# x1 of four token tiles kept in SBUF, loads tied to tiles, and stores in the order of their loads, in an S4 + gMLP block

## The chip, the cores and the metric

The kernel runs on one core of one Trainium2 chip. The metric is the device time of one execution in microseconds, the median over the runs that were taken.

## What is computed

One block with two parts, on x of 2048 tokens by 576 channels. The first part adds an S4 long convolution to x, with a kernel made from complex poles (128 states a channel); the second adds a gated MLP that mixes along the tokens.

```python
h = layernorm(x) * (1 + ca) + sa                 # sa..gb: silu(c) @ w_mod
x = x + ga * S4(h)                               # x after this line is "x1"
h = layernorm(x) * (1 + cb) + sb
z = gelu(h @ w_in)                               # 576 -> 4608
z1, z2 = z[:, :2304], layernorm(z[:, 2304:])
g = w_sp @ z2 + b_sp[:, None]                    # 2048 x 2048 over the tokens
x = x + gb * ((z1 * g) @ w_out)                  # 2304 -> 576
```

## The kernel before

Matrices of the MLP are split into two float16 parts each (high and low), and every product is three matmuls: high x high, high x low, low x high. The rows are in an order of tokens that the convolution likes, in 16 tiles of 128 tokens.

Instructions are recorded in program order, and a scheduler places them on the engines by its own estimate of times. An instruction that goes through `pin` (`keep_in_program_order`) is held in the order in which it was written. Each engine runs its own list in order; SyncE (SP) and GpSimd (POOL) mostly issue DMAs, and an issue that has to wait holds up all that stand behind it in that queue.

**SSM.** The convolution runs by channel chunks: four of 128 channels and one of 64 (`chan(c)`). At its end, `y_load(c, q)` loads v (from `v_d`) and x of four tiles (quarter q) and `y_unit(c, q)` multiplies, adds x in place (line 507) and stores x1 to the DRAM tensor `x1_d` (line 508). The last 64 columns of x1 stay in SBUF in `x1l`, too.

**First MLP phase** (`phase_a`, lines 922 to 983). For each of 16 tiles: `ln2_rows` loads x1 (line 862, tile x1t), takes its mean and variance (line 851) and normalises it; `ln2_cols` transposes it (line 877) into nt, which is stored to `n2_d` (line 884); `z2_mm` multiplies nt with the second half of w_in, which stays in SBUF as wz (line 899), and applies GELU (line 900), in three groups per tile of up to 28 matmuls, each with one of four PSUM buffers; `z2_stats` (ending in line 908) and `z2_parts` (lines 917 to 920) normalise z2 and store its two parts (zhl) to `z2_d`.

On the side, `side_win` runs at tiles 2, 4, 6, 8 and 10: it loads 512 columns of the first half of w_in (tile wst), squares them for a scale (line 705), sums over partitions with a matmul (line 726), splits them into wso (lines 690 and 695) and stores wso to `win_d` (line 830), 128 columns at a time. Columns of w_sp are loaded (wsst, line 835), normed (line 773) and split (wsp) in other tiles.

**Second MLP phase** (`phase_b`, from line 1064). For each quarter q of the output tokens and each of 18 groups f of 128 hidden channels: `z1_unit` loads 128 columns of w_in (wf, line 995, three buffers) and multiplies them with the normalised rows n2 of the quarter (line 1009, 14 matmuls), running four units ahead of `g_unit`; `g_unit` loads h2 of the group, the two parts of normalised z2 of all tokens (z2f, 1 MB, line 1017, two buffers), and multiplies it with the quarter's w_sp (lines 1021 to 1023, 48 matmuls), and VectorE gates it with z1. After the 18 groups `out_unit` makes the output of four tiles (lines 1055 to 1057, 432 matmuls in all), while the next quarter's w_sp is loaded and split.

Of the kernel before, what the change touches and what calls it, by code (L numbers as in the profile page):

```python
# [18 lines left out]
D = 576  # L19
# [99 lines left out]
def ssm(tc, I, x1_d, consts_s, dram, mod_d, mlp):  # L119
# [5 lines left out]
    with ExitStack() as ctx:  # L125
# [535 lines left out]
class Mlp:  # L661
    def __init__(self, tc, ctx, I, x1_d, dram, mod_d, acc, out):
        self.tc, self.I, self.x1_d, self.mod_d, self.acc, self.out = tc, I, x1_d, mod_d, acc, out
        self.ctx = ctx
        self.win_d = dram.tile([18, 128, 10, 128], F16, name="win_d")
        self.z2_d = dram.tile([18, 128, 16, 2, 128], F16, name="z2_d")
        self.n2_d = dram.tile([4, 128, 9, 512], F16, name="n2_d")
        self.wts, self.wss = {}, {}
# [11 lines left out]
    def win_load(self, t, c0, n):  # L680
        S, I = self.tc.nc.sync, self.I
        S.dma_start(t[:, 0:4, :n], I["w_in"][:512, c0:c0 + n].rearrange("(k p) n -> p k n", p=128))
        for h in range(2):
            S.dma_start(t[64 * h:64 * h + 64, 4, :n], I["w_in"][512:, c0:c0 + n])

# [13 lines left out]

    def win_norm(self, q, t, junk, n):  # L700

        nc = self.tc.nc
        V, A = nc.vector, nc.scalar
        wcol = self.wcol
        A.activation(junk, t[:, :, :n], AF.Square, accum_out=self.acc[:, q:q + 1])
# [4 lines left out]
    def win_split(self, q, t, dst, n, act=False):  # L710
# [3 lines left out]
        V.tensor_scalar(dst[:, 8, :n], t[:, 4, :n], s, None, op0=ALU.mult)  # L714
        V.scalar_tensor_tensor(dst[:64, 9, :n], t[:64, 4, :n], s[:64], dst[:64, 8, :n], op0=ALU.mult, op1=ALU.subtract)

# [12 lines left out]
    def start(self):  # L729
# [36 lines left out]
    def start_split(self, q):  # L766
        n = min(512, FH - 512 * q)
        self.win_split(5 + q, self.wts.pop(q), self.wz[:, :, 512 * q:512 * q + n], n, act=True)

# [48 lines left out]


    def side_win(self, q):  # L820
        V, S, ap = self.tc.nc.vector, self.tc.nc.sync, self.ap
        n = min(512, FH - 512 * q)
        o = ap.tile([128, 10, 512], F16, name="wso", bufs=1)
        V.memset(o[64:, 9, :n], 0.0)
# [19 lines left out]
    def stats(self, pool, x, nch):  # L844
# [10 lines left out]
        return mv[:, 0:1], r  # L855

    def ln2_rows(self, b):

        nc, ap = self.tc.nc, self.ap
        V, S = nc.vector, nc.sync  # L860
# [61 lines left out]
    def phase_a(self):  # L922
        self.nts, self.ns, self.zs, self.zn, self.wsp = {}, {}, {}, {}, {}
        ap = self.ap = self.pool(self.c2, "ap", 2)
# [3 lines left out]
        self.zp = self.pool(self.c2, "zp", 2)  # L928
        self.wp = self.pool(self.ctx, "wp", 20, side="right")
        self.fp = self.pool(self.ctx, "fp", 1, side="right")  # L930
# [55 lines left out]
    def z1_rows(self, q):  # L986
        nc, pool = self.tc.nc, self.bp if q % 2 else self.fp
        self.n2[q] = pool.tile([128, 9, 512], F16, name="n2q", bufs=1)
        nc.sync.dma_start(self.n2[q], self.n2_d[q])
        self.bsp[q] = pool.tile([128, 512], F32, name="bsp", bufs=1)  # L990
        nc.sync.dma_start(self.bsp[q], self.I["b_sp"][512 * q:512 * q + 512].partition_broadcast(128))

    def z1_load(self, q, f):
        w = self.wfs[q, f] = self.fp.tile([128, 10, 128], F16, name="wf", bufs=3)
        self.tc.nc.sync.dma_start(w, self.win_d[f])

    def z1_unit(self, q, f):
# [10 lines left out]
        for i, (kn, kw, p) in enumerate(Z1):  # L1008
            nc.tensor.matmul(pm, w[:p, kw], self.n2[q][:p, kn], start=i == 0, stop=i == len(Z1) - 1)  # L1009
        z = self.z1s[q, f] = bp.tile([128, 512], F32, name="z1", bufs=24)  # L1010
        nc.scalar.activation(z, pm, AF.Gelu_apprx_tanh, scale=self.wcol(f // 4, INV_IN))

    def g_unit(self, q, f):
        nc, bp = self.tc.nc, self.bp
        V, A, T, S = nc.vector, nc.scalar, nc.tensor, nc.sync
        z2 = bp.tile([128, 16, 2, 128], F16, name="z2f")
        S.dma_start(z2, self.z2_d[f])
        pm = self.pb.tile([128, 512], F32, name="pg")
# [155 lines left out]
```

## Time and profile before

| | |
|---|---|
| median of 3 runs | 1951.33 us (1949.46 to 1952.16) |
| profiled execution | 1948.36 us |
| its span | 1946.6 us |
| busy TensorE | 1821.1 us (94%) |
| busy VectorE | 905.8 us (47%) |
| busy ScalarE | 636.3 us (33%) |
| mean granted TensorE clock | 0.974 |

Times in the rows are in us from the start of the span, mean durations in ns. Rows of the timeline give the start, the time that the engine was busy, the engine, line, operation, tiles and count, and in brackets the idle time before and what ended it. Rows of stretches give the length, then for each engine its busy time and instructions, then the granted clock, the share of the DMA engines and GB/s. Rows of waits give the sum, the number and the longest. Rows of DMA issues give the count, KB each and the median us from issue to landing.

### The profile page before, as it was taken

To read this page: it belongs to the slowest core of one execution; us is meant where nothing else is said; L and a number is where in the kernel's file an instruction comes from. 1 tells how busy PE (TensorE), PEld (TensorE's weight loads), DVE (VectorE), ACT (ScalarE), POOL (GpSimd) and SP (SyncE) were. 2 spreads that over 40 slices of the span, in tenths; PEclk is the share of its full clock that TensorE was granted. 3 is DMA by queue.
4 is the path that set the end of the run, shared out by engine and by line. 5 is a ranking of instruction groups with operands and counts; after the bars stand their busy time and mean duration, and the time that the engine had idled before them with its cause. 6 is when DMAs were issued, how large, how long until landed. Compare 5 with 4: busy or idle time off the path is not lost.

```text
span 1946.6 us, 28063 instructions
## 1 busy us (share of the span) xinstructions
PE 1821.1 (94%) x11634; PEld 936.3 (48%) x11634; DVE 905.8 (47%) x2015; ACT 636.3 (33%) x860; POOL 183.7 (9%) x245
## 2 busy tenths in 40 slices
PE   3778999985988999999999999999999999999998
PEld 1444555653433443444457444447444447444457
DVE  5987999748768973224234212134221225212121
ACT  3769999643456663121100001110011110001000
POOL 3121232331111210000000000000000000000000
PEclk9788999997999999999999999999999999999999
DMA  8668456897475655556533224433333423323211
GB/s 218 174 178 256 112 140 171 206 273 211 149 235 169 175 157 186 186 184 226 183 124 117 104 97 147 152 132 121 103 114 118 157 99 127 104 86 114 69 61 38
DMA packets 145103, 290.66 MB, mean 149 GB/s; under 512 B 21456, under 2 KB 74448, under 8 KB 134608
## 3 DMA queue, kind: packets, MB, share of 16 engines
q1 hardware_dynamic: 122672, 217.19, 34.9%
q0 software_dynamic: 20000, 66.97, 12.0%
q10 hardware_dynamic: 2304, 4.72, 0.6%
q8 instruction: 91, 1.49, 0.3%
q14 instruction: 36, 0.29, 0.0%
HBM read 219.38 MB, written 60.02 MB: 144 GB/s over the span
## 4 chain that ended last, share of the span: by engine, by line
PE 65%; DVE 6%; issue 5%; DMA 4%; ACT 2%; POOL 1%; SPq 1%; POOLq 0%; ACTq 0%; DVEq 0%
PE pg L1021 13%; PE pg L1022 13%; PE pg L1023 13%; PE pz L1009 10%; PE po L1055 4%; PE po L1057 4%; PE po L1056 4%; DMA x1t<-x_d 2%; PE ps L899 2%; DVE bs L851 1%; DMA win_d<-wso 1%; ACT zhl L918 1%; PE pk L468 1%; DVE wso L695 1%; PE pk L455 1%
## 5 line engine op out<-in xcount | busy, mean ns | idle before, releaser
L1021 PE MATMUL pg<-wsp,z2f 128*128 128x512 f16 x1152 | 437.5, 380 | 0.0
L1022 PE MATMUL pg<-wsp,z2f 128*128 128x512 f16 x1152 | 436.9, 379 | 0.0
L1023 PE MATMUL pg<-wsp,z2f 128*128 128x512 f16 x1152 | 436.9, 379 | 0.0
L1025 DVE SCALAR_TENSOR_TENSOR gt<-pg,sc,bsp 128x512 f32<-128x512 f32 x72 | 54.1, 751 | 666.0 <-PE pg L1023 665.9
L1029 ACT ACTIVATE z<-gt 128x512 f16<-128x512 f32 x72 | 45.3, 629 | 796.2 <-DVE gt L1027 796.2
L899 PE MATMUL ps<-wz,nt 128*128 128x512 f16 (+2 forms) x1120 | 245.7, 368 | 26.0 <-ACT z L900 21.6
L1009 PE MATMUL pz<-n2q,wf 128*128 128x512 f16 (+1 forms) x924 | 217.0, 380 | 0.0
L899 PEld LDWEIGHTS <-nt 128*128 128x128 f16 (+1 forms) x1120 | 107.1, 100 | 161.9 <-issue 79.5
L1021 PEld LDWEIGHTS <-z2f 128*128 128x128 f16 x1152 | 112.6, 98 | 142.1 <-issue 13.6
L1023 PEld LDWEIGHTS <-z2f 128*128 128x128 f16 x1152 | 112.7, 98 | 136.0
L1022 PEld LDWEIGHTS <-z2f 128*128 128x128 f16 x1152 | 112.8, 98 | 128.5
L1009 PEld LDWEIGHTS <-wf 128*128 128x128 f16 x1008 | 97.8, 98 | 144.0 <-issue 34.8
L1055 PE MATMUL po<-wout,z 128*128 128x288 f16 x576 | 164.9, 286 | 0.0
L1056 PE MATMUL po<-wout,z 128*128 128x288 f16 x576 | 164.9, 286 | 0.0
L1057 PE MATMUL po<-wout,z 128*128 128x288 f16 x576 | 164.9, 286 | 0.0
L1058 ACT ACTIVATE ot<-po 128x288 f32<-128x288 f32 x32 | 13.1, 410 | 196.2 <-PE po L1057 196.2
L1030 DVE TENSOR_TENSOR gt<-gt,z 128x512 f32<-128x512 f32 x72 | 49.8, 691 | 47.4 <-ACT z L1029 47.4
L900 ACT ACTIVATE z<-ps,sc 128x512 f32<-128x512 f32 (+1 forms) x80 | 50.3, 636 | 47.9 <-PE ps L899 47.7
L1055 PEld LDWEIGHTS <-z 128*128 128x128 f16 x576 | 56.4, 98 | 14.9 <-issue 0.7
L1056 PEld LDWEIGHTS <-z 128*128 128x128 f16 x576 | 56.4, 98 | 14.2
L1057 PEld LDWEIGHTS <-z 128*128 128x128 f16 x576 | 56.4, 98 | 14.2
L1059 DVE TENSOR_TENSOR ot<-ot,po 128x288 f32<-128x288 f32 x32 | 14.5, 452 | 101.1 <-ACT ot L1058 101.0
(254 smaller groups left out, 2374.3 us busy)
## 6 DMA issues: line engine op xcount, KB each, us to landing
z2f<-z_d SPq DMA_DIRECT2D x72, 1024.0 KB, 4.8
wsst<-in_w_spT SPq DMA_DIRECT2D x64, 512.0 KB, 4.1
wf<-win_d SPq DMA_DIRECT2D x72, 320.0 KB, 2.9
z_d<-zhl POOLq DMA_DIRECT2D x16, 1152.0 KB, 7.2
u_d<-st1o POOLq DMA_DIRECT2D x16, 576.0 KB, 4.1
u<-u_d SPq DMA_DIRECT2D x36, 256.0 KB, 4.9
us<-ue POOLq DMA_DIRECT2D x72, 128.0 KB, 4.6
v_d<-v POOLq DMA_DIRECT2D x36, 256.0 KB, 3.7
```

Of the source, the lines that this page charges most:

```text
L899: nc.tensor.matmul(pm[:, h, :n], nt[:p, kn], self.wz[:p, kw, c0:c0 + n], start=i == 0, stop=i == len(PRE) - 1)
L900: nc.scalar.activation(z[:, c0:c0 + n], pm[:, h, :n], AF.Gelu_apprx_tanh, scale=self.wcol(5 + q + h, INV_IN))
L1009: nc.tensor.matmul(pm, w[:p, kw], self.n2[q][:p, kn], start=i == 0, stop=i == len(Z1) - 1)
L1021: T.matmul(pm, z2[:, st, 0], w[:, 0], start=st == 0, stop=False)
L1022: T.matmul(pm, z2[:, st, 0], w[:, 1], start=False, stop=False)
L1023: T.matmul(pm, z2[:, st, 1], w[:, 0], start=False, stop=st == 15)
L1025: V.scalar_tensor_tensor(t, pm, self.qcol(q, INV_SP), self.bsp[q], op0=ALU.mult, op1=ALU.add)
L1029: A.activation(p[:, 0], t, AF.Copy)
L1030: V.tensor_tensor(t, t, p[:, 0], op=ALU.subtract)
L1055: T.matmul(pa[:, :288], p[:, 0, ts], self.wout[:, f, 0, hs], start=f == 0, stop=False)
L1056: T.matmul(pa[:, :288], p[:, 0, ts], self.wout[:, f, 1, hs], start=False, stop=f == 17)
L1057: T.matmul(pl[:, :288], p[:, 1, ts], self.wout[:, f, 0, hs], start=f == 0, stop=f == 17)
```

## The change

x1 of the first four tiles (quarter 0) is gathered in `x1f`, SBUF that a zhl buffer takes over later (zhl gets its two buffers from two pools in turn, `zp` and `xz`). The last two chunks of quarter 0 are added there in place, and its first 384 columns are loaded from `x1_d` in one DMA before. `ln2_rows` of these tiles reads `x1f`; for the others `x1_load` issues the load two tiles ahead, pinned, at the end of `ln2_rows`. `side_win` gets its w_in from `side_load`, one tile earlier and pinned; its square and its split on ScalarE are pinned, and the split is made in pieces of 128 columns, so that wso and `win_d` have the same order in memory. `n2_d` is stored tile by tile in the order of nt, and the z1 matmuls read four runs of 128 columns from it. The loads of n2, b_sp and wf for z1 are pinned. h2 (z2f) is loaded from GpSimd's queue instead of SP's.

```diff
 def y_load(c, q):
-            if c == NC - 1:
+            if c >= NC - 2 and q == 0:
+                xb = mlp.x1f[:, :, chan(c)]
+            elif c == NC - 1:
                 xb = mlp.x1l[:, bs]
...
-        self.n2_d = dram.tile([4, 128, 9, 512], F16, name="n2_d")
+        self.n2_d = dram.tile([4, 128, 4, 9, 128], F16, name="n2_d")
...
 def win_norm(self, q, t, junk, n, pin=False):
-        A.activation(junk, t[:, :, :n], AF.Square, accum_out=self.acc[:, q:q + 1])
+        i = A.activation(junk, t[:, :, :n], AF.Square, accum_out=self.acc[:, q:q + 1])
+        if pin:
+            self.pin(i)
...
 def win_split(self, q, t, dst, act=False, pin=False):
-        self.split(dst[:, 0:4, :n], dst[:, 4:8, :n], t[:, 0:4, :n], s, act)
+        for j in range(dst.shape[2] if len(dst.shape) == 4 else 0):
+            self.split(dst[:, 0:4, j], dst[:, 4:8, j], t[:, 0:4, j], s, act, pin)
+        if len(dst.shape) == 3:
+            self.split(dst[:, 0:4], dst[:, 4:8], t[:, 0:4], s, act, pin)
...
 def start(self):
-        S.dma_start(self.x1l, I["x"][:, :, D - CHL:])
+        S.dma_start(self.x1l[:, 4:], I["x"][:, 4:, D - CHL:])
+        self.xz = self.pool(self.c2, "xz", 1)
+        x1f = self.xz.tile([128, 18, 2, 128], F16, name="zhl").rearrange("p f h c -> p (f h c)").bitcast(F32)
+        self.x1f = x1f.rearrange("p (b d) -> p b d", b=4)
+        S.dma_start(self.x1f[:, :, 384:], I["x"][:, :4, 384:])
+        S.dma_start(self.x1f[:, :, :384], self.x1_d[:4, :, :384].rearrange("b p d -> p b d"))
...
+    def side_load(self, q):
+        t = self.wts["in", q] = self.stg.tile([128, 5, 512], F32, name="wst")
+        return self.win_load(t, 512 * q, min(512, FH - 512 * q))
 def side_win(self, q):
-        o = ap.tile([128, 10, 512], F16, name="wso", bufs=1)
-        V.memset(o[64:, 9, :n], 0.0)
-        t = self.stg.tile([128, 5, 512], F32, name="wst")
-        self.win_load(t, 512 * q, n)
-        self.win_norm(q, t, o[:, 0:5, :n], n)
-        self.win_split(q, t, o, n, act=True)
+        o, t = self.wso, self.wts.pop(("in", q))
+        self.win_norm(q, t, o.rearrange(...)[...], n, pin=True)
+        self.win_split(q, t[...].rearrange("p k (j c) -> p k j c", c=128),
+                       o[:, :n // 128].rearrange("p j k c -> p k j c"), act=True, pin=True)
         for j in range(n // 128):
-            self.tc.nc.gpsimd.dma_start(self.win_d[4 * q + j], o[:, :, 128 * j:128 * j + 128])
+            self.tc.nc.gpsimd.dma_start(self.win_d[4 * q + j], o[:, j])
...
+    def x1_load(self, b):
+        xt = self.xts[b] = self.ap.tile([128, D], F32, name="x1t")
+        self.pin(self.tc.nc.sync.dma_start(xt[:, :D - CHL], self.x1_d[b, :, :D - CHL]))
 def ln2_rows(self, b):
-        xt = ap.tile([128, D], F32, name="x1t")
-        S.dma_start(xt[:, :D - CHL], self.x1_d[b, :, :D - CHL])
-        V.tensor_copy(xt[:, D - CHL:], self.x1l[:, b])
+        if b < 4:
+            xt = self.x1f[:, b]
+        else:
+            xt = self.xts.pop(b)
+            V.tensor_copy(xt[:, D - CHL:], self.x1l[:, b])
...
+        if 4 <= b + 2 < 16:
+            self.x1_load(b + 2)
 def ln2_cols(self, b):
-        nc.gpsimd.dma_start(self.n2_d[b // 4, :, :, 128 * (b % 4):128 * (b % 4) + 128], nt)
+        nc.gpsimd.dma_start(self.n2_d[b // 4, :, b % 4], nt)
 def z2_parts(self, b):
-        o = self.zp.tile([128, 18, 2, 128], F16, name="zhl")
+        o = (self.xz if b % 2 else self.zp).tile([128, 18, 2, 128], F16, name="zhl", bufs=1)
 def phase_a(self):
         for q in range(5):
+            loads[1 + 2 * q].append((self.side_load, q))
             sides[2 + 2 * q].append((self.side_win, q))
...
 def z1_load(self, q, f):
-        self.tc.nc.sync.dma_start(w, self.win_d[f])
+        self.pin(self.tc.nc.sync.dma_start(w, self.win_d[f]))
 def z1_unit(self, q, f):
-            nc.tensor.matmul(pm, w[:p, kw], self.n2[q][:p, kn], start=i == 0, stop=i == len(Z1) - 1)
+            nc.tensor.matmul(pm.rearrange("p (t c) -> p t c", t=4), w[:p, kw], self.n2[q][:p, :, kn], start=i == 0, stop=i == len(Z1) - 1)
 def g_unit(self, q, f):
-        S.dma_start(z2, self.z2_d[f])
+        nc.gpsimd.dma_start(z2, self.z2_d[f])
```

More of the change, by code (lines that the diff above doesn't have):

```diff
@@ L683, in win_load @@
         for h in range(2):
-            S.dma_start(t[64 * h:64 * h + 64, 4, :n], I["w_in"][512:, c0:c0 + n])
+            i = S.dma_start(t[64 * h:64 * h + 64, 4, :n], I["w_in"][512:, c0:c0 + n])
+        return i
     def split(self, hi, lo, src, s, act=False, pin=False):
@@ L698, in wcol, with win_norm @@
         return self.col(48 + 4 * q + i)
-    def win_norm(self, q, t, junk, n):
+    def win_norm(self, q, t, junk, n, pin=False):
         nc = self.tc.nc
@@ L708, in win_norm, with win_split @@
         V.tensor_tensor(wcol(q, INV_IN), wcol(q, I_W), self.col(I_H), op=ALU.mult)
-    def win_split(self, q, t, dst, n, act=False):
+    def win_split(self, q, t, dst, act=False, pin=False):
         V = self.tc.nc.vector
         s = self.wcol(q, S_W)
-        self.split(dst[:, 0:4, :n], dst[:, 4:8, :n], t[:, 0:4, :n], s, act)
-        V.tensor_scalar(dst[:, 8, :n], t[:, 4, :n], s, None, op0=ALU.mult)
-        V.scalar_tensor_tensor(dst[:64, 9, :n], t[:64, 4, :n], s[:64], dst[:64, 8, :n], op0=ALU.mult, op1=ALU.subtract)
+        for j in range(dst.shape[2] if len(dst.shape) == 4 else 0):
+            self.split(dst[:, 0:4, j], dst[:, 4:8, j], t[:, 0:4, j], s, act, pin)
+        if len(dst.shape) == 3:
+            self.split(dst[:, 0:4], dst[:, 4:8], t[:, 0:4], s, act, pin)
+        V.tensor_scalar(dst[:, 8], t[:, 4], s, None, op0=ALU.mult)
+        V.scalar_tensor_tensor(dst[:64, 9], t[:64, 4], s[:64], dst[:64, 8], op0=ALU.mult, op1=ALU.subtract)
     def total(self, dst, c0, n, ps=None):
@@ L767, in start_split @@
         n = min(512, FH - 512 * q)
-        self.win_split(5 + q, self.wts.pop(q), self.wz[:, :, 512 * q:512 * q + n], n, act=True)
+        self.win_split(5 + q, self.wts.pop(q)[:, :, :n], self.wz[:, :, 512 * q:512 * q + n], act=True)
     def norm_sp(self, q, i):
@@ L855, in stats @@
         return mv[:, 0:1], r
+    def x1_load(self, b):
+        xt = self.xts[b] = self.ap.tile([128, D], F32, name="x1t")
+        self.pin(self.tc.nc.sync.dma_start(xt[:, :D - CHL], self.x1_d[b, :, :D - CHL]))
     def ln2_rows(self, b):
         nc, ap = self.tc.nc, self.ap
[L860 to L863 removed]
+        V = nc.vector
+        if b < 4:
[3 more added lines that the diff above has]
+            V.tensor_copy(xt[:, D - CHL:], self.x1l[:, b])
         m, r = self.stats(ap, xt, 2)
@@ L922, in phase_a @@
     def phase_a(self):
-        self.nts, self.ns, self.zs, self.zn, self.wsp = {}, {}, {}, {}, {}
+        nc = self.tc.nc
+        self.nts, self.ns, self.xts, self.zs, self.zn, self.wsp = {}, {}, {}, {}, {}, {}
         ap = self.ap = self.pool(self.c2, "ap", 2)
@@ L929, in phase_a @@
         self.wp = self.pool(self.ctx, "wp", 20, side="right")
+        self.wso = ap.tile([128, 4, 10, 128], F16, name="wso", bufs=1)
+        nc.vector.memset(self.wso[64:, :, 9], 0.0)
         self.fp = self.pool(self.ctx, "fp", 1, side="right")
@@ L987, in z1_rows @@
         nc, pool = self.tc.nc, self.bp if q % 2 else self.fp
-        self.n2[q] = pool.tile([128, 9, 512], F16, name="n2q", bufs=1)
-        nc.sync.dma_start(self.n2[q], self.n2_d[q])
+        self.n2[q] = pool.tile([128, 4, 9, 128], F16, name="n2q", bufs=1)
+        self.pin(nc.sync.dma_start(self.n2[q], self.n2_d[q]))
         self.bsp[q] = pool.tile([128, 512], F32, name="bsp", bufs=1)
-        nc.sync.dma_start(self.bsp[q], self.I["b_sp"][512 * q:512 * q + 512].partition_broadcast(128))
+        self.pin(nc.sync.dma_start(self.bsp[q], self.I["b_sp"][512 * q:512 * q + 512].partition_broadcast(128)))
     def z1_load(self, q, f):
         w = self.wfs[q, f] = self.fp.tile([128, 10, 128], F16, name="wf", bufs=3)
-        self.tc.nc.sync.dma_start(w, self.win_d[f])
+        self.pin(self.tc.nc.sync.dma_start(w, self.win_d[f]))
     def z1_unit(self, q, f):
```

3 lines of the change are left out of this document (2 added, 1 removed).

## The prediction

> **What bounds the kernel now.** I read the page first, then busy time by stretches, then the waits and the order of instructions at the places where TensorE stands still. The profiled execution took 1948.36 us, 1.8 us more than its span; the median of the three runs shown, 1951.33 us, lies 3.0 us above it, and the sum below is made against the 1948.36.
>
> ```profile
> span 1946.6 us, 28063 instructions
> ```
>
> ```profile
> PE   3778999985988999999999999999999999999998
> ```
>
> One digit is 48.7 us. From the seventeenth slice on (about 780 us) TensorE is full: that is the second phase of the MLP, where only extra work or a new wait can move the end. Ahead of it are two holes that this change touches: slices 9 to 13, where the SSM ends and the first phase of the MLP begins, and that phase itself, up to about 770 us. The first 200 us have the largest hole, but the change does not touch them.
>
> The first phase computes z2 for 16 token tiles. I cut it at the transposes (line 877), in stretches of two tiles:
>
> ```profile
> core 0: us, PE busy (x) PEld busy (x) DVE busy (x) ACT busy (x) POOL busy (x), PEclk, DMA share, GB/s
> 405.00:455.00 50.00, 33.68 (x268) 24.22 (x268) 24.11 (x58) 15.22 (x18) 14.26 (x19) 0.82 1.05 297
> ...
> 512.69:556.50 43.81, 35.58 (x153) 15.28 (x152) 28.90 (x92) 22.89 (x28) 8.16 (x8) 0.88 0.65 215
> 556.50:592.43 35.93, 31.20 (x154) 14.27 (x153) 29.49 (x94) 22.79 (x26) 8.17 (x8) 1.00 0.65 196
> 592.43:630.57 38.14, 32.74 (x153) 14.62 (x153) 30.23 (x94) 23.87 (x28) 8.13 (x8) 0.96 0.62 174
> 630.57:661.74 31.17, 30.92 (x154) 14.32 (x153) 28.00 (x89) 18.99 (x24) 8.15 (x8) 1.00 0.68 185
> 661.74:693.42 31.68, 31.42 (x155) 14.46 (x155) 29.75 (x105) 20.37 (x27) 6.27 (x6) 1.00 0.54 148
> ```
>
> Five pairs with the same number of matmuls take 43.8, 35.9, 38.1, 31.2 and 31.7 us. The last two show what a pair costs when TensorE is the bound. The first three lose 12.6, 4.7 and 6.9 us against 31.2, together 24.3 us, partly as idle time and partly as a lower granted clock (0.88 and 0.96). Why they lose it stands in the waits between 464 and 746 us:
>
> ```profile
> ACT z L917 <- DVE nm L908: 41.0, 14, 6.0
> ...
> PE ps L899 <- ACT z L900: 21.6, 10, 4.9
> ...
> DVE bs L851 <- DMA x1t<-x_d: 13.8, 4, 4.2
> ...
> ACT wso L705 <- DMA wst<-in_w_in: 4.9, 1, 4.9
> ```
>
> TensorE waits 21.6 us for ScalarE to empty PSUM; ScalarE waits for the statistics of VectorE (41.0) and for w_in (4.9); VectorE waits 13.8 us for x1. So loads that come late, behind other things in SP's queue, are what three of the pairs pay for.
>
> **The change part by part.** *x1 of the first four tiles in SBUF.* Today tile 0 is loaded back from DRAM after the last store of x1:
>
> ```profile
> 448.95 0.27 DVE L824 MEMSET wso<- 64x256 uint32 x1
> 455.43 1.18 DVE L851 BATCH_NORM_STATS2 bs<-x1t 128x6 f32<-128x288 f32 x3 [6.21 <-DMA x1t<-x_d]
> ```
>
> ```profile
> 461.35 1.33 PE L877 MATMUL ps<-ident,n 128*128 128x128 f32 x5 [13.17 <-DVE rq L651]
> ```
>
> VectorE idles 6.2 us until x1t lands, and works 5.9 us until TensorE can transpose. In the built program the last chunks of the first four tiles are added in place and the statistics follow the last addition directly, so the 6.2 us go; the 5.9 stay. Against that stands the added load of the first 384 columns of four tiles (786 KB) in a stretch where the DMA engines are fully taken (row 405:455: share 1.05, 297 GB/s): 2.6 us if all of it delays the last loads of v. Something is given back: one x input fewer has to wait for a buffer in SP's queue there. Ends: -8 and -2 us. I take **-5**, nearer to the wait that I can read. What is late next is the third w_in slice, already in the same order.
>
> *Loads one or two tiles ahead, stores in load order.* x1t is issued two tiles ahead and w_in one tile ahead, each held in its place in the program; w_in goes out in runs of 2560 bytes instead of 256. The waits for x1 (13.8) and w_in (4.9) are what makes the first three pairs long; at 31.2 us each they would give back 24.3 us. But the built program also puts ScalarE's work on a w_in slice together: square, one scaling of z, four splits, where a tile lay between square and split before.
>
> ```profile
> L918 ACT ACTIVATE zhl<-z 128x2304 f16<-128x2304 f32 x15 | 31.7, 2113 | 0.1
> ```
>
> ```profile
> L690 ACT ACTIVATE wsp<-wsst,sc 128x512 f16<-128x512 f32 x16 | 10.2, 718 | 0.0
> L690 ACT ACTIVATE wso<-wst,sc 128x2048 f16<-128x2048 f32 (+1 forms) x5 | 9.2, 1831 | 8.6 <-DVE sc L634 8.6
> ```
>
> ```profile
> 498.02 14.74 PE L899 MATMUL ps<-wz,nt 128*128 128x256 f16 x70
> ```
>
> Four splits of 128x512 at 718 ns are 2.9 us for one of some 2.0. The splits need a sum that TensorE makes only after 28 further matmuls (28 of full width: 6.5 us; the 70 of a tile, 14 of them of half width, take 14.74). Walking one such tile from the end of its last matmul group: square until 3, scaling of z from about 8 (VectorE's order has the sum ahead of the statistics) to 10.3, splits to 13.2, a norm of w_sp to 14.2, one GELU, zhl (2.1 us by its row) and the second GELU until 17.5. TensorE has four PSUM buffers and wants the first back at 13.8, or, if the buffer of the sum is taken instead, at 15.6. So a w_in tile costs between 0 and 3.6 us more; I take 2 and there are five of them: 10 us. Sum of this part: -24.3 + 10 = **-14**; ends -27 (some of the gaps before 512 us go too) and -3 (3.6 each, and a little of the gain lost).
>
> *h2 of the second phase loaded by GpSimd instead of SP.* At the phase boundary SP stands in front of the first h2 tile (z2f, waiting for the last store), with the next w_in columns (wf) behind it:
>
> ```profile
> 766.03 0.32 SPq L1017 DMA_DIRECT2D z2f<-z_d  x1
> 766.45 0.85 SPq L995 DMA_DIRECT2D wf<-win_d  x2
> ```
>
> ```profile
> 765.64 3.30 PE L1009 MATMUL pz<-n2q,wf 128*128 128x512 f16 x14
> 771.65 8.22 PE L1009 MATMUL po<-n2q,wf 128*128 128x512 f16 x28 [2.71 <-DMA wf<-win_d]
> ```
>
> TensorE waits 2.7 us and then runs 28 matmuls in 8.22 us, where two units of 14 take 6.6. With z2f in GpSimd's queue wf is issued as soon as its buffer is free, so 2.7 + 1.6 = **-4.3** (ends -4.3 and 0). Behind the first z2f on GpSimd nothing else is queued but later z2f.
>
> *w_in columns of the second phase held in program order.* Here I see a new wait. In the built program the wf load of unit 22 (and of 40 and 58, once at each change of quarter) comes behind all but the first two loads of w_sp of the next quarter, and TensorE's order has that unit after 187 of the 432 output matmuls.
>
> ```profile
> 1014.60 12.75 SPq L835 DMA_DIRECT2D wsst<-in_w_spT  x5
> 1030.35 0.34 SPq L1046 DMA_DIRECT2D xo<-x_d  x1
> 1031.01 7.83 SPq L835 DMA_DIRECT2D wsst<-in_w_spT  x3
> ```
>
> ```profile
> 995.13 3.12 PE pz L1009 x14
> 1008.72 3.12 PE pz L1009 x14
> ```
>
> ```profile
> 1075.23 3.12 PE pz L1009 x14
> ```
>
> ```profile
> z2f<-z_d SPq DMA_DIRECT2D x72, 1024.0 KB, 4.8
> ...
> wf<-win_d SPq DMA_DIRECT2D x72, 320.0 KB, 2.9
> ...
> win_d<-wso POOLq DMA_DIRECT2D x18, 320.0 KB, 7.1
> ```
>
> One step of h2 and z1 takes 1008.72 - 995.13 = 13.6 us; the step with the output matmuls 66.5, so these take 52.9 us and 187 of them 22.9. Without the z1 unit in front they start at 1008.7, and unit 22 is due at 1031.6. The sixth of these w_sp loads is issued at 1031.0 now (it waits for the fourth split of its own stretch, which does not move), wf follows it and lands 2.9 us later, at 1034.3: a stall of 2.7 us, three times, **+8**. Ends 0 (no store delays the splits) and +15 (xo holds it up as well). Nothing hides it, as TensorE is full there.
>
> *Edits at nothing.* z1 now reads its moving operand as four runs of 128 columns. No matmul in this trace reads so; an output matmul of 288 columns takes 52.9/432 = 122 ns and one of 512 in the h2 step some (13.6 - 3.2)/48 = 217 ns, both 0.42 ns a column, so a start costs little: 0 to +4 us for 1008 matmuls, taken as 0. The n2 store in order and the alternate zhl pool change no wait that ends last.
>
> A rule of the Trainium skill speaks against loading z2f through GpSimd. First the rows: z2f through SP lands in 4.8 us; GpSimd's stores of win_d take 7.1 and are issued while VectorE is at work. It is requested when the step before has read its buffer, 13.6 us ahead of use, so 7.1 us is hidden, and so would be 12. The Trainium skill, "SBUF — State Buffer", section "Summary: rules for kernel authors", says to issue a transfer that must hide under VectorE work from ACT or SP, because descriptors made by GpSimd starve while VectorE is in its fast modes. By that rule alone z2f would come late; the 7.1 us row, a store, does not show starvation, and no row shows a load of this size on this queue.
>
> Sum: -5 - 14 - 4.3 + 8 = -15.3 us, or 1933.1 for the profiled execution and, 3 us up, about **1936** for the median. All ends added: -39.3 to +14.
>
> **The rivals.** *All of the gain.* If the built order of ScalarE costs nothing and the stalls at the quarters don't come (the rows above let the one be 0 and the other a matter of 3 us), -6.2 - 24.3 - 4.3 = -34.8 us: 1916. For it: the fourth pair shows a w_in tile at 31.2 us. Against: that tile had its split a tile later.
>
> *The loads stay late.* Held in program order, an x1t load can now sit in SP's queue behind a w_in load that waits for its staging buffer, so that the change doesn't do what it says. Then the second part shrinks from -14 to about 0, and -1.3 is left: 1950.
>
> Against it: two tiles are 31 us of lead, and the longest wait for x1t today is 4.2.
>
> *z2f late: slower.* Place: every step of the second phase. The step waits for all that the landing takes over 13.6 us (13.6 - 3.2 = 10.4 in the first six, where no z1 unit lies between). The nearest row on this queue, win_d, has 7.1 as its median; at 14.1 us, about twice that, the loss is 0.5 x 66 + 6 x 3.7 = 55 us against the gain of 15.3: 1991. It decides from about 13 us on: there the first six steps alone cost 16. By the skill's rule above this is what would happen; the rows give it little.
>
> **How the numbers follow.** The forecast gets 0.56, all of the gain 0.13, late loads 0.12, z2f late 0.09; 0.10 is left for a larger cost of the pinned orders, where w_in tiles and quarters both stand at their bad ends: -5 - 3 - 4.3 + 15 = 2.7 us slower, or 1954. The range goes from 1914, just past the first rival, to 1954, and leaves out z2f late and what lies beyond the two ends. Faster by over 0.2% (3.9 us, about what a measurement of this kernel can tell from no change) is 0.56 + 0.13 and half of the late-load case: 0.75; within it the other half and a little of the bad ends: 0.08; slower 0.17.
>
> **What would show it.** Right: no wait of VectorE for x1t above 1 us and the transposes of tile 0 some 5 to 6 us after the last addition of x1; pairs of tiles at 31 to 34 us; no wait for wf behind z2f at the phase boundary; a wait of 1 to 5 us for wf inside each block of output matmuls. Wrong: pairs still at 36 to 44 us; h2 matmuls waiting for z2f; z1 matmuls above 380 ns; the additions of x1 ending later than now.

## The result and the profile after

The changed kernel takes 1969.88 us (median of 4 runs, 1968.88 to 1973.8) against 1950.39 us for the kernel before in the same comparison: a ratio of 1.0105, interval 1.0086 to 1.0123. I had forecast 1936 us, with a range up to 1954. It became 19.5 us slower. The profiled executions stand at 1968.88 and 1948.36 us, 20.5 apart.

The waits of the first phase, after (engine, line, what for: sum, number, longest; the same code has a line number up to 26 higher than before):

```profile
DVE bs L865 <- DMA x1t<-x_d: 16.6, 8, 4.2
...
PE ps L921 <- ACT z L922: 14.5, 12, 4.3
...
PE ps L734 <- ACT wso L708: 13.3, 5, 2.9
```

The last row is new. TensorE's sum matmul (L734, L726 before) waits for ScalarE's square of the w_in slice in each of the five w_in tiles. VectorE's wait for x1t did not go: 16.6 us in place of 13.8. The timeline of TensorE and of ScalarE in one w_in tile shows how the new wait comes about (start, busy, and in brackets the idle time before):

```profile
513.59 0.77 PE L899 MATMUL ps<-ident,n 128*128 128x128 f32 x5
514.19 0.38 PE L921 MATMUL ps<-wz,nt 128*128 128x256 f16 x2
517.36 4.80 PE L921 MATMUL ps<-wz,nt 128*128 128x512 f16 x26 [2.79 <-ACT z L922]
525.04 0.38 PE L734 MATMUL ps<-acc,ones 128*128 128x1 f32 x2 [2.88 <-ACT wso L708]
525.28 8.20 PE L921 MATMUL ps<-wz,nt 128*128 128x512 f16 x28
```

```profile
522.20 0.47 ACT L922 ACTIVATE z<-ps,sc 128x256 f32<-128x256 f32 x1 [0.83 <-PE ps L921]
522.57 2.33 ACT L708 ACTIVATE wso<-wst 128x2560 f16<-128x2560 f32 x1
524.80 0.19 ACT L708 ACTIVATION_READ_ACCUMULATOR wso<-wst 128x1 f32 x1
```

The square is held behind the GELU of the tile's last group (522.20), which itself needs the 28 matmuls just made. The sum matmul stands directly behind those 28. So TensorE stands still for the whole length of the square, and the 28 matmuls behind it take 8.20 us where the prediction counted 6.5. In the kernel before, the sum matmul has the same place, with nothing between it and the matmuls ahead of it, but there the square of that slice was made at 484.3, long before:

```profile
516.95 7.59 PE L899 MATMUL ps<-wz,nt 128*128 128x512 f16 x26 [3.28 <-ACT z L900]
524.47 0.38 PE L726 MATMUL ps<-acc,ones 128*128 128x1 f32 x2
524.72 13.09 PE L899 MATMUL ps<-wz,nt 128*128 128x512 f16 x56
```

In the second phase the wait at the change of a quarter is there as drawn, here the second of three, on SP and on TensorE; and one that I had not drawn stands in the first quarter:

```profile
1336.34 2.74 SPq L849 DMA_DIRECT2D wsst<-in_w_spT  x2
1339.13 0.46 SPq L1021 DMA_DIRECT2D wf<-win_d  x1
```

```profile
1343.66 4.97 PE L1035 MATMUL pz<-n2q,wf 128*128 128x512 f16 x14 [3.33 <-DMA wf<-win_d]
```

```profile
812.54 42.61 SPq L790 DMA_DIRECT2D wsst<-in_w_out  x10
855.25 0.66 SPq L1021 DMA_DIRECT2D wf<-win_d  x1
```

wf is issued behind the w_sp loads, and TensorE waits 3.33 us for it. At 855.25 it is issued behind ten loads of w_out, which SP took 42.6 us to place.

**Where the 20.5 us are.** I cut each profiled execution at four places: ScalarE's first v (L479), the first transposes, the first z1 matmul, the first h2 matmul. The rows of the first cut, before and after, and of the last one, after:

```profile
197.07 0.57 ACT L479 ACTIVATE v<-pk 128x512 f32<-128x512 f32 x1
```

```profile
201.10 0.58 ACT L479 ACTIVATE v<-pk 128x512 f32<-128x512 f32 x1
```

```profile
788.41 0.39 PE L1047 MATMUL pg<-wsp,z2f 128*128 128x512 f16 x1
```

| us | to the first v | to the first transposes | first phase (to z1) | to the first h2 matmul | to the end |
|---|---|---|---|---|---|
| before | 197.07 | 264.28 | 284.90 | 36.78 | 1163.57 |
| after | 201.10 | 261.36 | 291.99 | 33.96 | 1178.69 |
| difference | +4.0 | -2.9 | +7.1 | -2.8 | +15.1 |

The +4.0 are not the change's: over the fifteen profiled executions of this study the first column lies between 197.1 and 201.4, for kernels with the change's parts and without (e4, which differs from the kernel before only far behind, has 197.95; e8, with no x1f, 200.40; e5, with all the change's loads, 197.50). The other columns come from one execution each, and they scatter too. In the first phase two kernels that are alike there are close (284.90 and e4's 285.45, e2's 266.78 and e3's 267.14). To the first transposes the nine kernels without x1f lie between 262.9 and 265.6. To the first h2 matmul the seven with h2 on SP fall into two groups, 36.4 to 36.9 and, in e8 and e11, 35.1 to 35.2. I read from the columns where a part acts, and from the medians how much it is worth.

### The profile page after: what moved, and what is told of

It is laid out like the page before. It is cut to its first block, busy times and chain, and to the rows that moved or that the text cites. A ratio compares the mean times of both kernels' runs of the same rounds, so it can differ in the third digit from the quotient of the medians.

```text
span 1967.1 us, 28126 instructions
## 1 busy us (share of the span) xinstructions
PE 1829.9 (93%) x11634; PEld 939.3 (48%) x11634; DVE 907.2 (46%) x2020; ACT 640.8 (33%) x873; POOL 208.2 (11%) x317
## 3 DMA queue, kind: packets, MB, share of 16 engines
q0 software_dynamic: 29824, 142.47, 21.6%
## 4 chain that ended last, share of the span: by engine, by line
PE 64%; DVE 8%; DMA 6%; ACT 3%; issue 2%; SPq 1%; ACTq 0%; DVEq 0%
PE pg L1047 13%; PE pg L1048 12%; PE pg L1049 12%; PE pz L1035 11%; PE ps L921 3%; PE po L1082 2%; PE po L1083 2%; PE po L1081 2%; DMA x1t<-x_d 2%; DMA wf<-win_d 2%; DVE bs L865 2%; DVE wsp L698 1%; DMA wsst<-in_w_spT 1%; PE pk L468 1%; ACT zhl L940 1%
## 5 line engine op out<-in xcount | busy, mean ns | idle before, releaser
L921 PE MATMUL ps<-wz,nt 128*128 128x512 f16 (+1 forms) x1120 | 248.4, 370 | 17.2 <-ACT z L922 14.5
L921 PEld LDWEIGHTS <-nt 128*128 128x128 f16 x1120 | 107.3, 100 | 155.0 <-issue 73.5
L1047 PEld LDWEIGHTS <-z2f 128*128 128x128 f16 x1152 | 112.6, 98 | 142.0 <-issue 13.3
L1043 POOL DMA_DIRECT2D z2f<-z_d x72 | 38.3, 532 | 1082.4 <-PE pg L1049 1006.9
L1037 ACT ACTIVATE z<-pz,sc 128x512 f32<-128x512 f32 x66 | 44.9, 680 | 83.7 <-PE pz L1035 83.6
L1085 DVE TENSOR_TENSOR ot<-ot,po 128x288 f32<-128x288 f32 x32 | 14.5, 452 | 116.7 <-ACT ot L1084 111.5
L1082 PEld LDWEIGHTS <-z 128*128 128x128 f16 x576 | 56.4, 98 | 15.2 <-issue 0.7
```

The source lines that it names most:

```text
L921: nc.tensor.matmul(pm[:, h, :n], nt[:p, kn], self.wz[:p, kw, c0:c0 + n], start=i == 0, stop=i == len(PRE) - 1)
L1047: T.matmul(pm, z2[:, st, 0], w[:, 0], start=st == 0, stop=False)
L1082: T.matmul(pa[:, :288], p[:, 0, ts], self.wout[:, f, 1, hs], start=False, stop=f == 17)
```

## The experiments

Each ratio is to the kernel before, run beside it on the same chip. Differences to the changed kernel, or between two experiments, are between medians of different sessions; the median of the kernel before moved between 1948.19 and 1950.48 us from one session to the next.

**e1: wf not held.**

```diff
-        self.pin(self.tc.nc.sync.dma_start(w, self.win_d[f]))
+        self.tc.nc.sync.dma_start(w, self.win_d[f])
```

> The changed kernel, but the wf loads are no longer held in program order (one pin taken off); everything else as in the change. In the built order each wf load stands ahead of the w_sp loads of the next quarter again, and ahead of the ten w_out loads. Theory 1 (SP's order): the five waits of TensorE for wf after the first step of h2 go, 2.5 us behind the w_out loads and 12.1 us at the three quarter changes (3.16, 5.18, 3.76 by the step times), so about 14.6 us less than the changed kernel: 1955 us, and z1 units of 22, 40, 58 come ahead of the output matmuls without a wait. Theory 2 (h2 through GpSimd makes all other loads land later, wf 4.6 us in place of 2.9): the waits move but stay, 1966 to 1970 us. A risk in both: three wf loads now stand in the middle of the first phase in front of x1t loads; a wait of VectorE for x1t there of some us would show it.

Measured: 1955.47 us, ratio 1.0027 (1.0011 to 1.0044), 14.4 less than the changed kernel. From the first h2 matmul to the end 1164.11 us in place of 1178.69; every quarter change takes 66.5 us again, as before. Theory 1 holds, and h2 through GpSimd takes no part in it. The first phase of its profiled execution is 296.76 us, 4.8 more than after. That is not the risk that I named: VectorE waits less for x1t than after (15.5 us against 16.6), and TensorE stands still as long (31.9 us against 31.3); its matmuls take 264.85 us in place of 260.68, at a granted clock of 0.94 in place of 0.96. The medians differ by about what the second phase alone gives, so I do not count it.

**e2: the square not held.**

```diff
-        self.win_norm(q, t, o.rearrange(...)[...], n, pin=True)
+        self.win_norm(q, t, o.rearrange(...)[...], n)
```

> The changed kernel, but the square of a w_in slice on ScalarE is no longer held in program order (the splits still are). In the built order the square then comes about half a tile earlier, ahead of the GELUs of the tile. Theory 1: the five waits of TensorE's sum matmul for the square (13.3 us, four of 2.88 and one of 1.81) go, and with them part of the lower clock that follows them (28 matmuls in 8.20 us in place of 6.52): 13 to 17 us less, 1953 to 1957 us. Theory 2 (ScalarE has too much to do in a w_in tile, in whatever order): the waits move to the GELUs and the total stays within 3 us of the changed kernel, 1967 to 1972 us.

Measured: 1943.93 us, ratio 0.9969 (0.9957 to 0.9981): 26 us less than the changed kernel, more than theory 1 had. The first phase takes 266.78 us in place of 291.99. TensorE at the same place:

```profile
511.01 5.32 PE L921 MATMUL ps<-wz,nt 128*128 128x256 f16 x28
516.27 0.38 PE L734 MATMUL ps<-acc,ones 128*128 128x1 f32 x2
516.51 6.52 PE L921 MATMUL ps<-wz,nt 128*128 128x512 f16 x28
```

The sum matmul no longer waits, the 28 matmuls behind it take 6.52 us, and over the whole first phase TensorE waits 8.1 us for GELUs where it waited 14.5:

```profile
PE ps L921 <- ACT z L922: 8.1, 9, 3.2
```

The sum is 13.3 us of waits for the square, 6.4 us of waits for GELUs, and matmuls that are shorter at a higher clock: busy time and clock in that stretch, after and in e2 (length, then TensorE's busy time, and behind the engines the granted clock):

```profile
462.46:754.45 291.99, 260.68 (x1219) 117.87 (x1219) 226.68 (x719) 172.67 (x211) 36.88 (x49) 0.96 0.50 167
```

```profile
459.19:725.97 266.78, 254.83 (x1218) 116.69 (x1219) 223.03 (x719) 171.39 (x211) 36.77 (x49) 0.98 0.55 182
```

That is 5.9 us of the 25.2; the rest is TensorE standing still.

**e3: neither wf nor the square and the splits held.** Both edits above, and `act=True, pin=True` of the split becomes `act=True`.

> The changed kernel without the pins on wf, and without those on the square and the splits of w_in. Theory 1: the sum of the two single edits, 14.6 and 13 to 17 us less than the changed kernel: 1938 to 1942 us, which is below the kernel before (1950) and near the time that I had predicted (1936). Theory 2: both waits come back in another place, 1962 to 1970 us.

Measured: 1928.45 us, ratio 0.9882 (0.9862 to 0.9902): 41.4 less than the changed kernel, about the two single edits added (14.4 and 26), and below theory 1, as e2 had been. It is faster than both kernels, by 21 us than the kernel before: the held orders of wf, the square and the splits had turned that gain into a loss of 19.5.

**e4: h2 through GpSimd, alone, in the kernel before.**

```diff
-        S.dma_start(z2, self.z2_d[f])
+        self.tc.nc.gpsimd.dma_start(z2, self.z2_d[f])
```

> The kernel before, with one edit: h2 of the second phase (z2f) is loaded from GpSimd's queue. Theory 1: the wait for wf behind z2f at the phase boundary goes (2.7 us and the slow matmuls behind it, 4.3 in all) and every step of h2 keeps its 13.59 us: 4 us less than before, 1946 us, landing about 5 us. Rival (transfers issued by GpSimd start late while VectorE works): steps of h2 above 13.6 us, over 1955 us.

Measured: 1949.03 us, ratio 0.9986 (0.9973 to 0.9999): a little less than before, at the limit of what can be told, and less than the 4 us of theory 1. The steps of h2 and z1 keep their 13.59 us, so the rival is out. The phase boundary is 34.57 us, 2.2 shorter, but TensorE's wait for wf did not go; it moved two units on and is 2.19 us in place of 2.71 (1.59 in the changed kernel). The rest, 1.7 us, are the slow matmuls that followed the wait before. They are missing in e8 and e11 as well, where h2 is on SP and the wait is as long as before; the rows are of e4 and of e8:

```profile
778.21 3.30 PE L1009 MATMUL pz<-n2q,wf 128*128 128x512 f16 x14 [2.19 <-DMA wf<-win_d]
```

```profile
781.94 6.53 PE L1022 MATMUL po<-n2q,wf 128*128 128x512 f16 x28 [2.78 <-DMA wf<-win_d]
```

So TensorE waits for wf with z2f out of SP's queue, too; what delays wf then stays open. z2f through GpSimd lands in 5.1 us:

```profile
z2f<-z_d POOLq DMA_DIRECT2D x72, 1024.0 KB, 5.1
```

**e5: a short square.**

```diff
-        i = A.activation(junk, t[:, :, :n], AF.Square, accum_out=...)
+        w = 32 if pin else n
+        i = A.activation(junk[:, :, :w], t[:, :, :w], AF.Square, accum_out=...)
```

> The changed kernel with all its pins, but the square of a w_in slice in the first phase runs over 32 of its 512 columns (the scale of the slice is then taken from those alone; the rest of the sum is left out). It keeps its place on ScalarE: behind the GELUs of the tile and ahead of the sum matmul on TensorE. Theory 1 (TensorE waits for the 2.3 us of the square, since the sum matmul stands directly behind the tile's matmuls): the waits of the sum matmul for it fall from 13.3 us to some 3 to 4, and the kernel to between 1944 (all that the free square gave) and 1960. Theory 2 (it is the late place of the square and of what follows it, staging freed late and loads behind it, not its length): 1963 to 1970 us.

Measured: 1948.21 us, ratio 0.9998 (0.9985 to 1.0011), 21.7 less than the changed kernel. The sum matmul still waits five times, but for 0.9 us at most:

```profile
PE ps L735 <- ACT wso L709: 4.4, 5, 0.9
```

The place is the same and the pin is the same; only the length differs, and with it go 17.5 us of the first phase (274.49). The shorter square also frees ScalarE's time behind it, and the scheduler put z2's scaling behind the splits, so not all of it is the wait; but theory 2 is out.

**e6: the square held, in the kernel before.**

```diff
-        A.activation(junk, t[:, :, :n], AF.Square, accum_out=...)
+        self.pin(A.activation(junk, t[:, :, :n], AF.Square, accum_out=...))
```

> The kernel before with one edit: the square of a w_in slice is held in program order on ScalarE, as in the change; loads, stores, h2 and wf as before. Theory 1 (that pin is the cost in the first phase): TensorE's sum matmul gets waits of up to 2.9 us in five tiles, and the kernel is 10 to 25 us slower than before, 1960 to 1975. Theory 2 (the pin costs only together with the loads tied to tiles or the split in pieces): 1946 to 1954 us.

Measured: 1972.24 us, ratio 1.0114 (1.0097 to 1.0132): 22.5 us slower by this one pin, within theory 1. The same five waits to the tenth, without any of the rest of the change:

```profile
PE ps L728 <- ACT wso L705: 13.3, 5, 2.9
```

**e7: e3 without x1f.** x1 of the first four tiles goes through `x1_load` like that of the others.

```diff
-            if c >= NC - 2 and q == 0:
-                xb = mlp.x1f[:, :, chan(c)]
-            elif c == NC - 1:
+            if c == NC - 1:
...
-        if b < 4:
-            xt = self.x1f[:, b]
-        else:
-            ...
+        xt = self.xts.pop(b)
+        V.tensor_copy(xt[:, D - CHL:], self.x1l[:, b])
```

> The changed kernel without the pins on wf, the square and the splits, and without x1f: x1 of the first four tiles goes through DRAM as before. Theory 1 (x1f is worth what the boundary shows, 3 to 4 us from the first v to the first transposes): 1931 to 1933 us, VectorE waiting some 6 us for the first x1t again. Theory 2 (what x1f saves at the boundary is lost elsewhere): 1927 to 1930 us.

Measured: 1933.2 us, ratio 0.991 (0.9893 to 0.9927), 4.8 more than e3. The medians differ by about what the boundary shows, within the scatter of four runs that lie between 1930.9 and 1937.58: from the first v to the first transposes the executions without x1f take 262.9 to 265.6 us (nine of them, mean 264.4), those with it 260.3 to 261.7 (six, mean 261.0).

**e8: the loads ahead, alone, in the kernel before.** `x1_load` and `side_load` as in the change, both held; nothing else.

```diff
-        xt = ap.tile([128, D], F32, name="x1t")
-        S.dma_start(xt[:, :D - CHL], self.x1_d[b, :, :D - CHL])
+        xt = self.xts.pop(b)
...
+        if b + 2 < 16:
+            self.x1_load(b + 2)
...
+            loads[1 + 2 * q].append((self.side_load, q))
```

> The kernel before with one edit: x1t is issued two tiles ahead and w_in one tile ahead, both held in program order on SP. Nothing else: stores, split, x1 of the first tiles, h2 and wf as before, the square free. Theory 1 (the late loads are what the first pairs of tiles pay for, as I had predicted, 24.3 us): 1926 to 1936 us. Theory 2 (the stores and loads in the same order in memory, win_d landing in 4.0 in place of 7.1 us, make much of the 18 us that the first phase gains without the pins): 1937 to 1947 us.

Measured: 1953.61 us, ratio 1.0023 (1.0009 to 1.0037): no gain at all, a small loss. Both theories missed. VectorE waits longer for x1t than before, 29.9 us against 20.0 when the wait for the first tile is counted in both (the 13.8 us leave it out), and SP's waits say what stands in front of it:

```profile
DVE bs L855 <- DMA x1t<-x_d: 29.9, 9, 7.5
```

```profile
SPq L839 <- ACT wsst L774: 66.7, 6, 22.8
...
SPq L839 <- ACT wsst L793: 18.9, 1, 18.9
```

A load of w_sp (L839) waits up to 22.8 us in SP's queue for its staging buffer, and x1t, held in program order, waits behind it. Nor did the ties bring any of these loads forward. On SP only this differs from the order before: two b_sp loads come later, one w_sp load comes ahead of an x1t load, and one x1t load comes three places later. In the kernel before the scheduler had placed x1t and w_in as early or earlier by itself, so e8 does not say what earlier loads would be worth.

**e9, e10, e11: the stores alone, in the kernel before.** e9 has both, e10 only n2, e11 only w_in; no load is tied and nothing is held. The store of w_in brings the split in pieces of 128 columns with it.

```diff
-        nc.gpsimd.dma_start(self.n2_d[b // 4, :, :, 128 * (b % 4):128 * (b % 4) + 128], nt)
+        nc.gpsimd.dma_start(self.n2_d[b // 4, :, b % 4], nt)
...
-            self.tc.nc.gpsimd.dma_start(self.win_d[4 * q + j], o[:, :, 128 * j:128 * j + 128])
+            self.tc.nc.gpsimd.dma_start(self.win_d[4 * q + j], o[:, j])
```

> The kernel before with the stores alone changed: n2 is stored tile by tile in the order of nt, and w_in in the order of wso, with the split in pieces of 128 columns; no load is tied, no pin added, x1 of the first tiles, h2 and wf as before. Loads ahead alone gave nothing (e8), and with the stores in order the first phase was 14 us shorter (e7). Theory 1 (the stores in order are what makes the first phase shorter, by themselves): from the first transposes to the first z1 matmul 268 to 274 us in place of 285, 1934 to 1940 us. Theory 2 (it takes both, earlier loads and the stores in order): 280 to 286 us there, 1945 to 1952.

> The kernel before with n2 alone stored tile by tile in the order of nt, and read by the z1 matmuls in four runs of 128 columns. The order of instructions on each engine is that of the kernel before, so only the transfers differ: runs of 2304 bytes in place of 256. Theory 1 (n2's stores count: n2 lands in 5.5 us in place of 7.6, GpSimd is free sooner, loads of x1t and w_in meet fewer small packets): 4 to 10 us less than before, 1940 to 1946. Theory 2 (nobody waits for n2's stores in the first phase): 1947 to 1952 us.

> The kernel before with w_in alone stored in the order of wso, the split in pieces of 128 columns. In the built order the square and the splits stand as in the free version of the change. Theory 1 (w_in's stores and the order of ScalarE's work that comes with the pieces count): most of what e9 gains over before, 6 to 14 us. Theory 2 (n2's stores count): within 3 us of before, 1947 to 1953 us.

Measured: e9 1942.47 us, ratio 0.9978 (0.9963 to 0.9993); e10 1944.87, 0.9985 (0.9968 to 1.0001); e11 1940.73, 0.9967 (0.9954 to 0.998). The first phase takes 275.5, 277.8 and 279.7 us in place of 284.9. So in these executions the stores alone shorten it, by 5 to 9 us, and e7, which has the loads tied on top of them (and h2 through GpSimd), has 271.2. That is between the two theories of e9. e10 has the order of instructions of the kernel before on every engine, so if its gain in that stretch is more than scatter it comes from the transfers, 6.8 us to land in place of 7.6 for n2; its total cannot be told from no change by its interval. e9 and e11 also have the same order on every engine and differ in n2's layout alone: e9 has the shorter first phase, e11 the lower median. So by the medians n2's layout is not shown to be worth anything, and w_in's, with the order of ScalarE's work that comes with it, is worth 0.2 to 0.3% by the ratios of e9 and e11. By which wait it shortens the first phase stays open: TensorE's waits for GELUs fall from 21.6 us to 17.3, 18.5 and 16.5, and those of VectorE for x1t fall in e9 and e11 only (13.8 to 4.2 and 3.7 in this stretch; 15.0 in e10). The Trainium skill ("DMA: Bandwidth & Descriptors", section "Why small descriptors are slow (HBM only)") gives small pieces to or from HBM a fixed extra cost each; the landing times agree with it in direction (n2 in e10 as above; w_in in e11 5.0 us in place of 7.1).

**e12, e13: x1t not held.** e12 is e8, e13 is e3, each with

```diff
-        self.pin(self.tc.nc.sync.dma_start(xt[:, :D - CHL], self.x1_d[b, :, :D - CHL]))
+        self.tc.nc.sync.dma_start(xt[:, :D - CHL], self.x1_d[b, :, :D - CHL])
```

> The kernel of e8 (before, with x1t two tiles and w_in one tile ahead), but only w_in's loads are held in program order; x1t may be placed freely. Theory 1 (in e8 x1t, held behind a w_sp load that waits 18.9 us for its buffer, comes late, 29.9 us of waits of VectorE in place of 13.8): the waits for x1t fall below 20 us, the stretch from the first transposes to the first z1 matmul from 292 to between 280 and 286, 1943 to 1950 us. Theory 2 (w_in's loads, in front of everything else at 1 MB each, make x1t late wherever it stands): 289 to 294 us there, 1951 to 1956.

> The kernel of e3 (the change without the pins on wf, square and splits), with x1t also free; w_in stays one tile ahead and held. Theory 1 (the pin on x1t costs what e12 shows): waits of VectorE for x1t below the 6.4 us of e3 and 1922 to 1927 us. Theory 2 (with the stores in order the loads land in time as they are): 1926 to 1931 us, the same as e3.

Measured: e12 1953.16 us, ratio 1.0008 (0.9992 to 1.0025); e13 1930.97, 0.9906 (0.9889 to 0.9923). e12 turned out to be the kernel before: its order of instructions is the same on every engine but for the two b_sp loads on SP, and so is its time, 285.7 us in the first phase and 23.8 us of waits for x1t (20.0 before). The scheduler put these loads in the same places with the edit as without it. Against it the pin on x1t in e8 costs 6 us of first phase in the profiled executions (291.9), as theory 1 had it, but theory 1's waits and total were missed and the medians of e8 and e12 are the same within 0.5 us; so that the pin on x1t is what e8 loses is not shown. In e13 freeing x1t gains nothing (2.5 us more than e3, with 10.1 us of waits for x1t in place of 6.4): theory 1 is out there.

## Why the prediction was wrong, step by step

| term | predicted (ends) | measured | from |
|---|---|---|---|
| x1f at the boundary | -5 (-8 to -2) | -2.9; -3.4 over all executions | columns; e7: 4.8 in all |
| loads ahead, stores in order | -14 (-27 to -3) | +7.1 | first phase, after |
| the same without the held square | | -18.1 | first phase, e2 |
| h2 off SP | -4.3 (-4.3 to 0) | -2.8; alone -2.2, of which 1.7 is clock | to the first h2 matmul; e4 |
| wf held at three quarter changes | +8 (0 to 15) | +12.1 | steps, below |
| wf held behind w_out's loads | not seen | +2.5 | steps |
| z1 from four runs of columns | 0 (0 to 4) | under 1 | to the end, e1, e3; 0.0 in e10 |

Of the 35.8 us between the sum (1933.1) and the profiled execution (1968.88), 21 stand in the second row and 6.6 in wf.

**The step that failed is the w_in tile**, "So a w_in tile costs between 0 and 3.6 us more; I take 2 and there are five of them". It cost 5.0: 291.99 - 266.78 = 25.2 us for five, where the sum had 10. In walking through that tile I had put the sum matmul behind 28 further matmuls, 6.5 us of cover for the square. It stands behind the 28 whose GELU the square waits for, so there was no cover: TensorE pays the 2.3 us of the square and 0.5 us of the GELU ahead of it and of handing over, then a lower clock, then a late chain of GELUs. The kernel before had the sum matmul in the same place, so its trace could have told me. e2 shows it by freeing the square, e5 by shortening it, and e6 by holding it in the kernel before. My bounds for that cost were worked out from PSUM buffers alone; a wait of TensorE itself was not among the ends.

**The gain beside it was about right in size, and its cause is not shown.** 24.3 us were read from the first three pairs of tiles and laid to late loads. Without the held square the phase is 18.1 us shorter than before, and these three pairs take 31.7, 32.1 and 32.2 us (e2), together 21.9 less than before:

```profile
510.41:542.09 31.68, 31.14 (x154) 14.20 (x153) 28.63 (x94) 22.09 (x31) 5.70 (x8) 1.00 0.70 242
542.09:574.20 32.11, 30.89 (x154) 14.20 (x153) 28.66 (x94) 22.78 (x29) 5.73 (x8) 1.00 0.67 224
574.20:606.37 32.17, 31.05 (x154) 14.20 (x153) 26.93 (x89) 20.38 (x27) 5.75 (x8) 1.00 0.61 199
```

By first phases, one execution each and in this order, the stores make 9.4 of the 17.8 us that e3 gains there (e9), the ties and what else e7 has 4.3, and x1f 4.0 (e3 against e7). The last two are uncertain by several us: e7's profiled execution was the slowest of its four, 4.4 us above its median. That the late loads were the cause is not borne out: with the stores in order and no load tied the waits for x1t fall to 4.2 us (e9), and e10 gains 7.1 us with waits of 15.0. Ties by themselves brought no load forward (e8, e12). The row "VectorE waits 13.8 us for x1" was true; in the changed kernel the waits are 16.6, with the pin on x1t kept and only the square free they are 4.7 (e2), so there it was the held square, not the pin alone, that kept x1 late.

**The wait at the quarter changes came as drawn.** I had a stall of 2.7 us for unit 22 behind the sixth w_sp load; it is 3.0, 3.3 and 3.6. The step times are 69.67, 71.69 and 70.27 us in place of 66.51, so 3.2, 5.2 and 3.8: in the second the 14 matmuls after the wait took 4.97 us where 3.30 is usual. What I did not look for is the same mechanism once more: wf behind w_out's loads, 2.5 us over two steps. e1 takes both away.

**The wait for wf at the phase boundary was laid to z2f in front of it, and taking z2f away did not remove it.** With z2f on GpSimd's queue it is still 1.59 us (after) and 2.19 (e4) in place of 2.71. The 1.7 us of slow matmuls behind it went, but they are also missing in e8 and e11, with h2 on SP: that part of the -2.8 is luck.

**The rivals.** That h2 through GpSimd would come late has fallen: 5.1 us to land against 4.8 through SP, and no step longer (e4). The rule of the Trainium skill that I had weighed there ("SBUF — State Buffer", section "Summary: rules for kernel authors") has descriptors made by GpSimd starve while VectorE is in its fast modes; this trace shows no sign of that, with VectorE busy for about a quarter of that phase (313.5 of 1178.7 us, after). No row says in which mode VectorE's operations ran, so the runs do not test the rule itself. "The loads stay late" came true in the waits (16.6 us for x1t after, against 13.8), and I gave it 0.12; but it is not what cost the 25.2 us. "All of the gain" did not come in any kernel: e3, without the costs, stays at 1928. No case of held orders reached 1970: the one that ended slower had both at their bad ends and came to 1954, since the end for the w_in tile was too near.

## What to carry to other kernels

When an instruction is held in program order, look at who waits for its result on the bottleneck engine, and count what stands between the two there: with nothing in between, its whole length was on the path here, in all five tiles. A pin on a load moves it to its place in the program, and behind all that is written ahead of it in that queue; it is early only if that is free. Whether a tie moves anything shows in the order that the engine runs: the ties of e8 and e12 moved nearly nothing. A bundle of edits should be taken apart before it is dropped: here the pins on wf, the square and the splits cost 41 us and hid a gain of 21.

## What the runs showed that I had not expected

A wait in the middle of the matmuls can cost more than its length. Behind the wait of 2.88 us in the tile shown above the granted clock is about half for 3.4 us. So the 28 matmuls there take 8.20 us in place of 6.52 (e2): 1.7 us more, half of 3.4.

```profile
525.28:533.42 8.14, 8.14 (x31) 2.99 (x30) 6.83 (x30) 7.16 (x10) 2.17 (x4) 0.79 0.21 82
525.64:529.05 3.41, 3.41 (x10) 1.22 (x8) 3.34 (x23) 2.79 (x2) 0.00 (x0) 0.51 0.00 0
```

It does not follow every wait, and the length alone does not decide. The three waits for wf at the quarter changes, 2.99, 3.33 and 3.59 us, each stand alone among full matmuls. Only the second is followed by a lower clock; here are the 14 matmuls behind each:

```profile
1042.48:1045.78 3.30, 3.30 (x15) 1.35 (x16) 2.88 (x6) 0.00 (x0) 0.00 (x0) 1.00 0.47 153
1343.66:1348.63 4.97, 4.97 (x15) 1.67 (x16) 2.85 (x6) 0.00 (x0) 0.00 (x0) 0.66 0.51 159
1646.78:1650.08 3.30, 3.30 (x15) 1.34 (x16) 3.27 (x7) 0.00 (x0) 0.00 (x0) 1.00 0.00 0
```

In the same way 26 matmuls take 7.59 us behind a wait of 3.28 us in the kernel before, and 4.80 us behind one of 2.79 us after. What decides between them the runs do not show.

Over the first phase the clock is lower where TensorE stands still more: 0.98 in e2, 0.96 after, and 0.93 in e6, where the same matmuls take 267.39 us in place of 258.24 in the kernel before, which differs by the pin alone:

```profile
464.35:770.56 306.21, 267.39 (x1219) 119.97 (x1219) 227.18 (x715) 170.39 (x198) 50.64 (x49) 0.93 0.54 159
```

The Trainium skill ("TensorE: Matmul & The Clock Gate", section "HAM oscillation — how this bites in real kernels") warns of idle gaps of TensorE above some 3.4 us. Here gaps of 2.88 and 3.33 us were followed by the lower clock, and one of 3.59 us was not.

And the first 200 us, which no version here alters in substance, differ by 4 us from one execution to the next, about the scatter of the totals: a term of that size cannot be read from one total. A stretch of the trace is better, but it too moves by 1.7 us with each such spell of the lower clock.
